# Making x with tokens on partitions and turning it by DMA transposes, in a fused linear-attention and bilinear feed-forward kernel

## The chip, the cores and the metric

One core of a Trainium2 chip runs the whole program. The metric is the device time of one execution in microseconds (us), by its median over several executions. All runs told here are of the fast state. Ratios are the mean time of one kernel's fast runs over that of the kernel before's fast runs of the same rounds, so they are not quite the ratio of the medians that I quote.

## The reference, cut to what matters

```python
def _attn_ref(q, k, v, g_norm):                      # 8 batches, 8 heads, 576 tokens, 64 dims
    kv = np.einsum('bhsd,bhse->bhde', k, v)
    out = np.einsum('bhsd,bhde->bhse', q, kv)
    rms = np.sqrt(np.mean(out * out, axis=-1, keepdims=True) + 1e-06)
    return out / rms * g_norm

def _moe_ref(x, w_a, w_b, w_out):                    # x: 4608 tokens x 512
    return ((x @ w_a) * (x @ w_b)) @ w_out           # 512 -> 1536 -> 512
```

x is the attention's output with the heads laid side by side. The feed-forward part contracts over x's 512 columns, so it wants x with columns on partitions and tokens along the free axis ("turned").

## The kernel before

Tokens go through the feed-forward part in nine strips of 512. While strip s (1 to 6) runs, the attention of batch s+1 is made between its matmuls, by `slot`. A step n below 12 of a strip is a unit: four matmuls for a, four for b, a ScalarE copy of a, a VectorE multiply of the two. Steps 12 to 15 are the output matmuls. x is made already turned, a pair of heads at a time, and so are its norms:

```python
        def x(self, p, i0):                      # x turned: columns on partitions
            for h in range(2):
                nc.tensor.matmul(P[:, i0 + h, 0:HF], lhsT=kvb[self.b % 2][:, p, :],
                                 rhs=self.qT[:, p, h * HF : (h + 1) * HF], start=True, stop=True)
        def psq(self, p, i0):                    # ScalarE: squares
            nc.scalar.activation(sq[p % 3], P[:, i0 : i0 + 2, 0:HF], AF.Square)
        def pss(self, p, i0, hs=(0, 1)):         # TensorE: sum over a head's 64 rows, on all rows
            for h in hs:
                nc.tensor.matmul(P[:, i0 + h, 0:HF], lhsT=ones, rhs=sq[p % 3][:, h, :], ...)
            ...                                  # ScalarE: 1/sqrt
        def pst(self, p, x0, hs=(0, 1)):         # VectorE: x * g * 1/rms
            ...
    def load_late(b):
        if b > EARLY:                            # GpSimd waits here for the q transpose of b-1
            nc.gpsimd.tensor_copy(gate, qT[(b - 1) % 2][0:1, 0, 0:1])
        ...                                      # six DMAs issued by GpSimd: q, k, v of batch b
    def transpose_q(b):
        nc.sync.dma_start_transpose(qT[b % 2], qs_d[b])
```

The sum over a head's rows runs across partitions, which is why it costs eight TensorE matmuls per batch.

Of the kernel before, what the change touches and what calls it, by code (L numbers as in the profile page):

```python
# [8 lines left out]
FP32 = mybir.dt.float32  # L9
BF16 = mybir.dt.bfloat16  # L10
AF = mybir.ActivationFunctionType
# [4 lines left out]
def kernel(  # L16
# [11 lines left out]
    nc = tc.nc  # L28

    B, H, S, D = q.shape  # L30
    d_model = H * D
    n_tok = B * S
    d_ff = moe_w_a.shape[1]
    KC = d_model // 128
    FC = d_ff // 128
    NP = H // 2
    HF = S // 2
    STRIP = 512
# [3 lines left out]
    EC, EP = 6, 96  # L42
# [6 lines left out]
    def sb(shape, dt, name):  # L49
        return pool.tile(shape, dt, name=name, tag=name)  # L50
# [11 lines left out]
    LC = S // 128  # L62
# [5 lines left out]
    kvs = [sb([128, NP, D], BF16, f"kvs{i}") for i in range(2)]  # L68

    kvb = [sb([128, NP, 128], BF16, f"kvb{i}") for i in range(2)]  # L70
    xt = [sb([128, n_tok], BF16, f"xt{i}") for i in range(KC)]
    abt = [[sb([128, STRIP], BF16, f"ab{i}_{f}") for f in range(FC)] for i in range(2)]
    a_sb = [sb([128, STRIP], BF16, f"asb{i}") for i in range(4)]
    sq = [sb([128, 2, HF], BF16, f"sq{i}") for i in range(3)]
    rs = [sb([128, 2, HF], FP32, f"rs{i}") for i in range(3)]
    o_sb = [sb([128, d_model], FP32, f"osb{i}") for i in range(4)]
    o_end = sb([128, d_model // 2], FP32, "o_end")
    ident = sb([128, 128], BF16, "ident")
# [3 lines left out]
    eps_t = sb([128, 1], FP32, "eps_t")  # L82
    warm = sb([128, 1], FP32, "warm")
    k32 = sb([EP, 2, EC, D], FP32, "k32")
    v32 = sb([EP, 2, EC, D], FP32, "v32")
    q32 = sb([EP, 2, EC, D], FP32, "q32")

    qc = sb([EP, EC, 2 * D], BF16, "qc")
    kc0 = sb([EP, EC, 2 * D], BF16, "kc0")
# [5 lines left out]
    P = psum.tile([128, 8, STRIP], FP32, name="P", tag="P")  # L95
# [27 lines left out]
    def load_late(b):  # L123
        if b > EARLY:

            nc.gpsimd.tensor_copy(gate, qT[(b - 1) % 2][0:1, 0, 0:1])  # L126
        d = qs_d[b].rearrange("t (h d) -> t h d", h=H)
        for hs in (slice(0, NP), slice(NP, H)):
            nc.gpsimd.dma_start(out=d[:, hs, :], in_=q[b, hs].rearrange("h t d -> t h d"))  # L129
        n = 128 * LC  # L130
        for t, src in ((ktl[b % 2], k), (vtl[b % 2], v)):
            nc.gpsimd.dma_start(
                out=t[:, :, 0:LC, :],
                in_=src[b, :, 0:n].rearrange("h (t c) d -> t h c d", c=LC),
            )
            nc.gpsimd.dma_start(
                out=t[0 : S - n, :, LC, :], in_=src[b, :, n:].rearrange("h t d -> t h d")
            )

    def transpose_q(b):  # L140
        nc.sync.dma_start_transpose(qT[b % 2], qs_d[b])


    class Attn:
# [75 lines left out]
        def pst(self, p, x0, hs=(0, 1)):  # L220
            for h in hs:
                t0 = self.b * S + h * HF
                nc.vector.scalar_tensor_tensor(  # L223
                    out=xt[p][:, t0 : t0 + HF],
                    in0=P[:, x0 + h, 0:HF],
                    scalar=g_col,
                    in1=rs[p % 3][:, h, :],
                    op0=ALU.mult,
                    op1=ALU.mult,
                )  # L230
# [10 lines left out]
                )  # L241


    class Unit:
        n = 0

# [5 lines left out]
        def mm(self, w, kcs):  # L252
            t0 = self.s * STRIP
            for kc in kcs:
                nc.tensor.matmul(  # L255
                    self.a if w is wa_t else self.b,
                    lhsT=w[:, kc, self.fc * 128 : (self.fc + 1) * 128],
                    rhs=xt[kc][:, t0 : t0 + STRIP],
                    start=(kc == KORD[0]),
                    stop=(kc == KORD[-1]),  # L260
                )
# [19 lines left out]
    def ffn_ab(s, fc, between=None):  # L281
        i = n_ab[0]
        n_ab[0] += 2
        u = Unit(s, fc, i % 3, (i + 1) % 3)
        u.part_a()
        if between:
            between()
        u.part_b()
# [38 lines left out]
    def ffn_o(s, g, i=O, between=None):  # L327
        o_mm(s, g, i, range(FC // 2))
        if between:
            between()  # L330
        o_mm(s, g, i, range(FC // 2, FC))
        o_out(s, g, i)
# [43 lines left out]
    X, SS = (4, 0), 6  # L376


    A = Attn(0)
# [9 lines left out]
    t = P[:, 2, :].bitcast(BF16)[:, 0:S].rearrange("q (c t) -> q c t", c=EC)  # L389
# [4 lines left out]
    for c in range(EC):  # L394
        nc.tensor.matmul(
            P[:, SS, 0 : 2 * D],
            lhsT=kc0[:, c, :],
            rhs=vc[:, c, :],
            start=(c == 0),
            stop=(c == EC - 1),  # L400
# [10 lines left out]
    for p in range(1, NP):  # L411
        i = X[p % 2]
# [38 lines left out]
    for fc in range(4, FC):  # L451
        ffn_ab(0, fc)


    A = Attn(1)
    h1, h2 = range(0, FC // 2), range(FC // 2, FC)
# [29 lines left out]
    def slot(A, s, n):  # L486

        kb = P[:, 7, 0 : NP * D].rearrange("q (p e) -> q p e", e=D)
        if s < 3:
            k0, xs, ss = 6, (7, 9.5, 12, 13.5), (8, 10.5, 12.5, 14)  # L490
        else:
            k0, xs, ss = 2, (4, 7, 10, 12), (5, 8, 11, 13)
        if n == k0:
            for p in range(NP):
                A.kv(p, kb[:, p, :])
            A.kv_out(slice(0, NP), kb)
        if n in xs:
            p = xs.index(n)
            A.x(p, X[0])
            A.psq(p, X[0])  # L500
        if n in ss:
            p = ss.index(n)
            A.pss(p, SS)
            A.pst(p, X[0])

    for s in range(1, N_STRIP - 1):
        b = s + 1
        A = Attn(b) if b < B else None
        for n in range(FC + 4):
            amid = (lambda n=n: slot(A, s, n - 0.5)) if A else None  # L510
            if n >= FC:
                i = O if n % 2 == 0 else n_ab[0] % 3
                n_ab[0] += n % 2
                ffn_o(s, n - FC, i, amid)
            elif s > 1 or n > 1:
                ffn_ab(s, n, amid)
            if A:
                slot(A, s, n)
            if n == 8 and b + 1 < B:
                if s > 1:  # L520
                    transpose_q(b + 1)
                    if b + 2 < B:
                        load_late(b + 2)
                else:
                    load_late(3)
        if s == 1:
            transpose_q(3)
            load_late(4)
# [43 lines left out]
```

## Time and profile before

| what | value | how to read it |
|---|---|---|
| median time | 322.1 us | 3 runs, 321.55 to 322.46, as known at the prediction; a fourth came with the result |
| span of the profiled run | 319.4 us | first to last instruction |
| TensorE busy | 98% | matmuls overlap, so take distances between starts |
| strip with attention | 33.90 us | strips 1 to 6, starts at 50.37, 84.27, 118.16 and so on |
| strip without | 31.08 us | strip 7 |
| GpSimd's issue of one batch's load | 7.2 us | nothing else runs on it meanwhile |

The lines themselves stand in the prediction below.

### The profile page before, as it was taken

What the parts mean: (1) busy time and instruction counts of PE and PEld (TensorE: products, weight loads), DVE (VectorE), ACT (ScalarE), POOL (GpSimd) and SP (SyncE); (2) the same over time, 40 slices, a digit from 0 to 9 for tenths busy, and PEclk for the clock granted to TensorE, in tenths of its full rate; (3) what the DMA queues carried; (4) which work ended last, traced back from release to release, by engine and by line L of the source; (5) the groups of instructions that cost most, each with busy time, mean ns of one, the idle gap of its engine ahead of it and who ended that gap; (6) DMA issues with size and microseconds to landing.
All of it is one profiled execution on the core that took longest, in us unless ns stands there. A gap on an engine that the chain in (4) does not pass through costs nothing.

```text
span 319.4 us, 4695 instructions
## 1 busy us (share of the span) xinstructions
PE 312.0 (98%) x1848; PEld 150.2 (47%) x1883; DVE 124.6 (39%) x218; ACT 125.3 (39%) x217; POOL 70.2 (22%) x94
## 2 busy tenths in 40 slices
PE   8899999999999999999999999999999999999995
PEld 3444454444445444444444444444544444444443
DVE  5543344444244333452245324532364243313421
ACT  3733165354335443542445225542454323123310
POOL 8944990070043080350070000000000000000000
PEclk9999999999999999999999999999999999999999
DMA  8999999999379999899499150003000200020002
GB/s 182 197 196 199 201 182 230 141 95 161 99 92 159 135 123 211 81 138 173 119 94 129 66 139 2 0 35 100 0 2 14 90 30 0 34 84 18 0 33 99
DMA packets 79308, 32.60 MB, mean 102 GB/s; under 512 B 49974, under 2 KB 74806, under 8 KB 79286
## 3 DMA queue, kind: packets, MB, share of 16 engines
q0 software_dynamic: 59120, 18.44, 53.0%
q1 hardware_dynamic: 19810, 13.44, 17.1%
q10 hardware_dynamic: 356, 0.43, 0.4%
q8 instruction: 14, 0.23, 0.3%
q14 instruction: 8, 0.07, 0.1%
HBM read 37.75 MB, written 12.98 MB: 159 GB/s over the span
## 4 chain that ended last, share of the span: by engine, by line
PE 93%; POOL 3%; DMA 2%; issue 1%; ACT 0%; POOLq 0%
PE P L255 58%; PE P L309 29%; PE P L209 2%; PE P L235 2%; DMA wb_t<-in_moe_w_b_dram 2%; PE P L158 2%; POOL vt L106 1%; POOL qt L106 1%; POOL kt L106 1%; PE P L182 0%; POOL wa_t L367 0%; POOL wb_t L367 0%; ACT o_end L540 0%; POOL ident masks.py:199 0%; POOL ident masks.py:197 0%
## 5 line engine op out<-in xcount | busy, mean ns | idle before, releaser
L273 DVE TENSOR_TENSOR ab<-P,asb 128x512 bf16<-128x512 f32 x108 | 74.5, 691 | 124.0 <-PE P L255 120.7
L255 PE MATMUL P<-xt,wa_t 128*128 128x512 bf16 x422 | 111.2, 379 | 0.9 <-issue 0.2
L255 PE MATMUL P<-xt,wb_t 128*128 128x512 bf16 x421 | 110.1, 379 | 0.3
L309 PE MATMUL P<-wo_t,ab 128*128 128x512 bf16 (+1 forms) x431 | 97.5, 373 | 0.7
L269 ACT CAST asb<-P 128x512 bf16<-128x512 f32 x108 | 63.0, 585 | 85.3 <-PE P L255 83.8
L255 PEld LDWEIGHTS <-wb_t 128*128 128x128 bf16 x432 | 42.3, 98 | 50.6 <-DMA wb_t<-in_moe_w_b_dram 0.5
L309 PEld LDWEIGHTS <-ab 128*128 128x128 bf16 x444 | 43.1, 98 | 45.4
L255 PEld LDWEIGHTS <-wa_t 128*128 128x128 bf16 x432 | 41.7, 98 | 45.1 <-issue 0.5
L223 DVE SCALAR_TENSOR_TENSOR xt<-P,g_col,rs 128x288 bf16<-128x288 f32 x64 | 30.1, 513 | 29.6 <-ACT rs L213 29.6
L205 ACT ACTIVATE sq<-P 128x576 bf16<-128x576 f32 x31 | 20.2, 650 | 25.1 <-PE P L235 23.2
L213 ACT ACTIVATE rs<-P,eps_t 128x576 f32<-128x576 f32 (+1 forms) x33 | 23.9, 727 | 14.9 <-PE P L209 14.6
L322 ACT COPY osb<-P 128x512 f32<-128x512 f32 x17 | 10.0, 586 | 46.0 <-PE P L309 43.6
L324 DVE COPY osb<-P 128x512 f32<-128x512 f32 x18 | 12.4, 691 | 26.9 <-PE P L309 26.8
L129 POOL DMA_DIRECT2D qs<-in_q_dram x12 | 19.6, 1636 | 2.2 <-issue 2.1
L126 POOL COPY gate<-qT 1x1 bf16<-1x1 bf16 x5 | 0.9, 176 | 83.2 <-DMA qT<-qs 83.2
L209 PE MATMUL P<-sq,ones 128*128 128x288 bf16 x64 | 13.2, 286 | 0.5 <-ACT sq L205 0.4
L235 PE MATMUL P<-qT,kvb 128*128 128x288 bf16 x56 | 11.4, 286 | 0.0
L169 ACT CAST kvb<-P 64x256 bf16<-64x256 f32 (+1 forms) x20 | 6.0, 301 | 11.1 <-PE P L158 11.0
L209 PEld LDWEIGHTS <-ones 128*128 128x128 bf16 x64 | 6.2, 98 | 7.5 <-issue 0.4
L235 PEld LDWEIGHTS <-kvb 128*128 128x128 bf16 x56 | 5.5, 98 | 6.0
L121 POOL DMA_DIRECT2D wo_t<-in_moe_w_out_dram x12 | 6.4, 530 | 6.7 <-DMA wb_t<-in_moe_w_b_dram 3.3
L337 PE MATMUL P<-zeros 128*128 128x512 bf16 x16 | 6.2, 532 | 1.2 <-DVE eps_t L352 1.2
(55 smaller groups left out, 82.6 us busy)
## 6 DMA issues: line engine op xcount, KB each, us to landing
out_dram<-osb SPq DMA_DIRECT2D x23, 256.0 KB, 2.0
qs<-in_q_dram POOLq DMA_DIRECT2D x12, 288.0 KB, 6.6
ktl<-in_k_dram POOLq DMA_DIRECT2D x6, 512.0 KB, 8.7
vtl<-in_v_dram POOLq DMA_DIRECT2D x6, 512.0 KB, 10.7
out_dram<-osb SPq DMA_DIRECT2D x13, 128.0 KB, 2.4
wo_t<-in_moe_w_out_dram POOLq DMA_DIRECT2D x12, 128.0 KB, 6.0
wa_t<-in_moe_w_a_dram POOLq DMA_DIRECT2D x5, 256.0 KB, 9.2
wb_t<-in_moe_w_b_dram POOLq DMA_DIRECT2D x5, 256.0 KB, 9.8
```

The lines of the kernel that those rows point to most:

```text
L129: nc.gpsimd.dma_start(out=d[:, hs, :], in_=q[b, hs].rearrange("h t d -> t h d"))
L205: nc.scalar.activation(sq[p % 3], P[:, i0 : i0 + 2, 0:HF], AF.Square)
L209: nc.tensor.matmul(P[:, i0 + h, 0:HF], lhsT=ones, rhs=sq[p % 3][:, h, :], start=True, stop=True)
L213: nc.scalar.activation(rs[p % 3][:, h0:h1, :], P[:, i0 + h0 : i0 + h1, 0:HF], AF.Abs_reciprocal_sqrt, bias=eps_t,)
L223: nc.vector.scalar_tensor_tensor(out=xt[p][:, t0 : t0 + HF], in0=P[:, x0 + h, 0:HF], scalar=g_col, in1=rs[p % 3][:, h, :], op0=ALU.mult, o ...
L235: nc.tensor.matmul(P[:, i0 + h, 0:HF], lhsT=kvb[self.b % 2][:, p, :], rhs=self.qT[:, p, h * HF : (h + 1) * HF], start=True, stop=True,)
L255: nc.tensor.matmul(self.a if w is wa_t else self.b, lhsT=w[:, kc, self.fc * 128 : (self.fc + 1) * 128], rhs=xt[kc][:, t0 : t0 + STRIP], st ...
L269: nc.scalar.copy(self.t, self.a)
L273: nc.vector.tensor_mul(abt[self.s % 2][self.fc], self.b, self.t)
L309: nc.tensor.matmul(P[:, i, e0:e1], lhsT=abt[s % 2][fc][:, g * 128 : (g + 1) * 128], rhs=wo_t[:, fc, e0:e1], start=(fc == 0), stop=(fc == F ...
L322: nc.scalar.copy(t, P[:, i, :])
L324: nc.vector.tensor_copy(t, P[:, i, :])
```

## The change

Its intent: with tokens on partitions, the sum over a head's 64 columns runs along the free axis. A VectorE reduce does it, and the eight sum matmuls go away; the x matmuls shrink to 128 columns. The price is that x comes out unturned, and a DMA transpose turns each chunk of 128 tokens. The core of the diff:

```diff
-    xt = [sb([128, n_tok], BF16, f"xt{i}") for i in range(KC)]
+    xt = sb([128, KC, n_tok], BF16, "xt")
...
+    q_x = sb([128, 2 * EC * D], FP32, "q_x")                  # q's first tile, used again
+    x_tok = q_x.bitcast(BF16).rearrange("p (c h d) -> p c h d", c=3, h=H)   # three buffers
...
+        def tx(self, c, i):
+            ...
+            for p in range(NP):
+                nc.tensor.matmul(P[0:n, i, p * 128 : (p + 1) * 128],
+                    lhsT=self.qT[:, p, t0 : t0 + n], rhs=kvb[self.b % 2][:, p, :], ...)
+            nc.scalar.activation(sqt[c % 2][0:n], P[0:n, i, :]..., AF.Square)
+        def tss(self, c):
+            nc.vector.reduce_sum(sst[c % 2][0:n], sqt[c % 2][0:n], axis=mybir.AxisListType.X)
+        def trs(self, c):
+            nc.scalar.activation(rst[c % 2][0:n], sst[c % 2][0:n], AF.Abs_reciprocal_sqrt, ...)
+            nc.gpsimd.tensor_mul(sqt[c % 2][0:n], <rst over columns>, <g_all over heads>)
+        def txt(self, c, i):
+            t = x_tok[:, c % 3]
+            nc.vector.tensor_mul(t[0:n], P[0:n, i, :]..., sqt[c % 2][0:n])
+            nc.sync.dma_start_transpose(xt[:, :, t0 : t0 + n], t[0:n]...)
...
+    nc.sync.dma_start(out=g_all, in_=g_norm.partition_broadcast(128))
...
-        if s < 3:
-            k0, xs, ss = 6, (7, 9.5, 12, 13.5), (8, 10.5, 12.5, 14)
-        else:
-            k0, xs, ss = 2, (4, 7, 10, 12), (5, 8, 11, 13)
+        k0 = {1: 5, 2: 3}.get(s, 2)
...
+        for c in range(LC + 1):                 # five chunks, one a unit
+            d = n - k0 - 1.5 - c
+            i = 4 + c % 3                       # three PSUM banks
+            # d == 0: tx, 0.5: tss, 1: trs, 2: txt
...
-            if n == 8 and b + 1 < B:            # (load_late(b + 2) at step 8; strip 1: load_late(3))
+            if s == 1 and n == 3:
+                load_late(3)
+            if s > 1 and b + 1 < B:
+                if n == 8:
+                    transpose_q(b + 1)
+                if n == 12 and b + 2 < B:
+                    load_late(b + 2)
```

`g_all` is the norm's weight on all partitions.

More of the change, by code (lines that the diff above doesn't have):

```diff
@@ L75 @@
     rs = [sb([128, 2, HF], FP32, f"rs{i}") for i in range(3)]
+    sqt = [sb([128, H, D], FP32, f"sqt{i}") for i in range(2)]
+    sst = [sb([128, H], FP32, f"sst{i}") for i in range(2)]
+    rst = [sb([128, H], FP32, f"rst{i}") for i in range(2)]
+    g_all = sb([128, D], FP32, "g_all")
     o_sb = [sb([128, d_model], FP32, f"osb{i}") for i in range(4)]
@@ L85 @@
     v32 = sb([EP, 2, EC, D], FP32, "v32")
-    q32 = sb([EP, 2, EC, D], FP32, "q32")
+    q_x = sb([128, 2 * EC * D], FP32, "q_x")
+    q32 = q_x[0:EP].rearrange("p (h c d) -> p h c d", h=2, c=EC)
+    x_tok = q_x.bitcast(BF16).rearrange("p (c h d) -> p c h d", c=3, h=H)
     qc = sb([EP, EC, 2 * D], BF16, "qc")
@@ L223, in pst @@
                 nc.vector.scalar_tensor_tensor(
-                    out=xt[p][:, t0 : t0 + HF],
+                    out=xt[:, p, t0 : t0 + HF],
                     in0=P[:, x0 + h, 0:HF],
@@ L241, in x @@
                 )
+        def tx(self, c, i):
+            t0 = c * 128
+            n = min(128, S - t0)
+            for p in range(NP):
+                nc.tensor.matmul(
+                    P[0:n, i, p * 128 : (p + 1) * 128],
+                    lhsT=self.qT[:, p, t0 : t0 + n],
+                    rhs=kvb[self.b % 2][:, p, :],
+                    start=True,
+                    stop=True,
+                )
+            nc.scalar.activation(
+                sqt[c % 2][0:n], P[0:n, i, :].rearrange("t (h d) -> t h d", h=H), AF.Square
+            )
+        def tss(self, c):
+            n = min(128, S - c * 128)
+            nc.vector.reduce_sum(sst[c % 2][0:n], sqt[c % 2][0:n], axis=mybir.AxisListType.X)
+        def trs(self, c):
+            n = min(128, S - c * 128)
+            nc.scalar.activation(
+                rst[c % 2][0:n],
+                sst[c % 2][0:n],
+                AF.Abs_reciprocal_sqrt,
+                bias=eps_t[0:n],
+                scale=1.0 / D,
+            )
+            nc.gpsimd.tensor_mul(
+                sqt[c % 2][0:n],
+                rst[c % 2][0:n].unsqueeze(2).to_broadcast([n, H, D]),
+                g_all[0:n].unsqueeze(1).to_broadcast([n, H, D]),
+            )
+        def txt(self, c, i):
+            t0 = c * 128
+            n = min(128, S - t0)
+            t = x_tok[:, c % 3]
+            nc.vector.tensor_mul(
+                t[0:n], P[0:n, i, :].rearrange("t (h d) -> t h d", h=H), sqt[c % 2][0:n]
+            )
+            t0 += self.b * S
+            nc.sync.dma_start_transpose(
+                xt[:, :, t0 : t0 + n], t[0:n].rearrange("t h d -> t (h d)")
+            )
     class Unit:
@@ L257, in mm @@
                     lhsT=w[:, kc, self.fc * 128 : (self.fc + 1) * 128],
-                    rhs=xt[kc][:, t0 : t0 + STRIP],
+                    rhs=xt[:, kc, t0 : t0 + STRIP],
                     start=(kc == KORD[0]),
@@ L496, in slot @@
             A.kv_out(slice(0, NP), kb)
-        if n in xs:
-            p = xs.index(n)
-            A.x(p, X[0])
-            A.psq(p, X[0])
-        if n in ss:
-            p = ss.index(n)
-            A.pss(p, SS)
-            A.pst(p, X[0])
+        for c in range(LC + 1):
+            d = n - k0 - 1.5 - c
+            i = 4 + c % 3
+            if d == 0:
+                A.tx(c, i)
+            elif d == 0.5:
+                A.tss(c)
+            elif d == 1:
+                A.trs(c)
+            elif d == 2:
+                A.txt(c, i)
     for s in range(1, N_STRIP - 1):
@@ L518 @@
                 slot(A, s, n)
-            if n == 8 and b + 1 < B:
-                if s > 1:
+            if s == 1 and n == 3:
+                load_late(3)
+            if s > 1 and b + 1 < B:
+                if n == 8:
                     transpose_q(b + 1)
-                    if b + 2 < B:
-                        load_late(b + 2)
-                else:
-                    load_late(3)
+                if n == 12 and b + 2 < B:
+                    load_late(b + 2)
         if s == 1:
```

## The prediction

> **What bounds the kernel now.** I read, in this order: the page's busy shares and its chain of work that ended last; the chain in order of time; the stretches table by strip (a strip is 512 tokens of the feed-forward part); the timelines of TensorE and of GpSimd.
>
> ```profile
> PE 312.0 (98%) x1848; PEld 150.2 (47%) x1883; DVE 124.6 (39%) x218; ACT 125.3 (39%) x217; POOL 70.2 (22%) x94
> ...
> PE 93%; POOL 3%; DMA 2%; issue 1%; ACT 0%; POOLq 0%
> ```
>
> TensorE is busy 98% and carries 93% of the chain; the rest is the start. So what counts is what TensorE issues, and whether it is made to wait. The stretches table has one row per strip; the first column is the strip's start and end, then its length:
>
> ```profile
> 118.33:152.22 33.89, 33.73 (x198) 16.28 (x200) 13.45 (x22) 14.39 (x24) 7.00 (x8) 1.00 1.26 151
> 152.22:186.12 33.90, 33.69 (x198) 16.29 (x200) 13.45 (x22) 14.39 (x24) 6.57 (x7) 1.00 0.73 102
> 253.92:285.00 31.08, 30.92 (x142) 14.10 (x144) 9.69 (x14) 8.19 (x14) 0.00 (x0) 1.00 0.09 35
> ```
>
> A strip that also carries the attention of the next batch takes 33.90 us, the strip without takes 31.08. Attention costs 2.82 us of a strip, and that is all that the change can touch. TensorE's timeline in such a strip (start, length, count) prices it:
>
> ```profile
> 123.44 0.82 PE L158 MATMUL P<-vtl,ktl 128*64 128x64 bf16 x40
> ...
> 125.93 1.03 PE L255 MATMUL P<-xt,wa_t 128*128 128x512 bf16 x4
> 126.79 1.03 PE L255 MATMUL P<-xt,wb_t 128*128 128x512 bf16 x4
> 127.66 0.41 PE L235 MATMUL P<-qT,kvb 128*128 128x288 bf16 x2
> 127.90 1.03 PE L255 MATMUL P<-xt,wa_t 128*128 128x512 bf16 x4
> ```
>
> Durations overlap, so I take starts. Eight 512-column matmuls start 1.73 us apart: 0.216 us each. Two 288-column ones take 127.90 - 127.66 = 0.24 us: 0.1225 each. The 40 of kv take 0.75 us to the next start (124.19). Check: 144 x 0.216 = 31.1; 16 x 0.1225 = 1.96 (8 for x, 8 for the sums of squares); 0.75; together 33.8 of 33.90. No gap is left, so TensorE waits for nobody in these strips.
>
> GpSimd's timeline at the load of batch 3, and 128-column matmuls that each have their own weights:
>
> ```profile
> 62.92 0.18 POOL L126 COPY gate<-qT 1x1 bf16<-1x1 bf16 x1 [15.02 <-DMA qT<-qs]
> 63.76 3.26 POOL L129 DMA_DIRECT2D qs<-in_q_dram  x2 [0.67 <-issue]
> 67.00 0.90 POOL L132 DMA_DIRECT2D ktl<-in_k_dram  x1
> 67.89 0.70 POOL L136 DMA_DIRECT2D ktl<-in_k_dram  x1
> 68.56 0.91 POOL L132 DMA_DIRECT2D vtl<-in_v_dram  x1
> 69.44 0.72 POOL L136 DMA_DIRECT2D vtl<-in_v_dram  x1
> ```
> ```profile
> 6.80 0.49 PE L395 MATMUL P<-vc,kc 96*128 96x128 bf16 x6 [0.18 <-ACT vc L387]
> ```
>
> GpSimd waits at its gate until the q transpose has landed, then spends 7.2 us issuing the load (62.92 to 70.16) and can do nothing else. The six 128-column matmuls last 0.49 us, of which the last lasts 0.218: (0.49 - 0.218) / 5 = 0.054 us from start to start, fresh weights included.
>
> **What the Trainium skill says.**
> 1. "TensorE: Matmul & The Clock Gate", section "Back-to-back issue gap": a lone matmul costs N/2.4 + 2.5 ns (56 ns for 128 columns), but about 81 ns for 128 and 131 ns for 512 in a stream of weight-load and matmul pairs. The trace has 216, 122.5 and 54 ns for 512, 288 and 128 columns, so it agrees with the formula and not with the stream figures. I take 0.056.
> 2. "GPSIMD Engine Reference", section 3.1: a two-input elementwise operation of 2048 fp32 takes 4497 ns. Scaled to 512 I estimate 1.2 us for the new multiply. No run here shows it yet. Section 4: two of GpSimd's cores make the descriptors of DMAs issued there, which agrees with the 7.2 us above.
> 3. "SBUF — State Buffer", section "Who interferes with whom": on trn2 a VectorE reduce never contends with GpSimd, nor does an instruction with at most one SBUF input. All new VectorE work is of those kinds. Nothing before shows it.
>
> **The change part by part.**
> Removed per batch from 2 to 7: 8 x-matmuls and 8 sum-matmuls, 16 x 0.1225 = 1.96 us of TensorE, all on the path; 4 squares of 650 ns and 4 roots of 741 ns on ScalarE (5.6 us); 8 VectorE multiplies of 513 ns (4.1 us).
>
> Added per batch: 5 chunks of tokens, each of 4 matmuls of 128 columns: 20 x 0.056 = 1.12 us of TensorE, on the path. The sums now go to a VectorE reduce, the norm to a small ScalarE root and a GpSimd multiply, x to a VectorE multiply out of PSUM, and the layout to a DMA transpose. Per chunk: VectorE 691 ns for the multiply (the row of the same shape, 128x512 out of PSUM) and an estimated 0.6 for the reduce (two copies of 512 and 256 columns take 691 and 426 ns, so 1.04 ns a column; 512 of them and some 60 ns); ScalarE an estimated 0.6 for the square (650 ns at 576 columns) and 0.2 for the root; GpSimd an estimated 1.2. All beside TensorE unless late.
>
> TensorE's ceiling on the gain: 6 x (1.96 - 1.12) = 5.0 us. I take off 0.5 for 30 new short groups between long matmuls (under 20 ns each, a choice): 4.5 us.
>
> Does the side work keep up? A unit (two groups of four matmuls) with a chunk lasts 1.73 + 0.22 = 1.95 us. In the three middle units VectorE has 0.69 + 0.69 + 0.6 = 1.98 us: just full. Following the first chunks by order: counting from the start of the unit with chunk 0, square done at 2.2, reduce at 3.4, root at 3.8, GpSimd at 5.1, x multiply about 5.4 to 6.1. Chunk 3 takes chunk 0's PSUM bank and wants it at 6.8. So 0.7 us of slack, and in the later strips no wait.
>
> In strip 1 GpSimd is not free. load_late(3) is now placed at step 3, ahead of the multiplies, but its gate still waits for q of batch 2, 62.92 us, so GpSimd issues until 70.16 and then multiplies until 71.4. In the old trace kv starts at 62.62; it is a unit earlier now, so chunk 0 runs at about 64.3, its root is there at 67, and chunk 3 wants the bank at about 70.2. The x multiply ends 71.4 + 0.1 + 0.7 = 72.2. TensorE waits about 2.1 us. In strip 2 the same load of batch 4 ends (98.7 in the old trace, shifted 1.4 by the above) at about 100.1; multiply and x end 102.1, bank wanted 101.9: 0.3 us. From strip 3 on the load is issued at step 12, past the multiplies: nothing.
>
> DMA transposes: q's 576x512 takes 4.8 to 11.2 us to land and 2.2 to 6.2 us of the queue's issue, so 128x512 should take an estimated 2 to 4 us. Strip s+1 wants its first chunks 7 units (13 us) after their issue or more. In strip 2 the q transpose of batch 4 stands ahead of chunk 2 on the same queue and waits for its load until about 104, so chunk 2 lands near 114, wanted at 119. Hidden.
>
> Sum: -4.5 + 2.1 + 0.3 = -2.1 us: 322.1 becomes 320.0 us.
>
> **The rivals.**
> A. Short matmuls are dearer than the formula. At 81 ns, 20 of them cost 1.62 us: the gain is 6 x 0.34 = 2.0, and with the 2.4 us of waits the result is 322.5. For: the skill's stream figure. Against: 54 ns in this trace, but only in one group of six.
> B. VectorE becomes the bound in the middle units. It is full by my sum, with 0.7 us of slack; a multiply of GpSimd above 2.2 us, or each of about eight hand-overs costing 0.1 us more than I counted, turns into a wait of 0.3 to 1 us in each of six strips: 322 to 326.
> C. Transposes come late: x at the start of strip 3, or a chunk's buffer held so long that VectorE stops. For: shares of 1.08 and 1.26 of DMA in strips 2 and 3, and a queue in order. Against: margins of 5 us and more. A wait of 3 us twice would give 326.
> D. No wait in strip 1, because the q transpose lands earlier or the multiply is not held: 317.5.
>
> **Range and chances.** A, B and C only add, D subtracts 2.4. I predict 320.0 us, 317.3 to 323.0 eight times in ten. 2% is 6.4 us. Faster than 315.7 is beyond TensorE's 5.0 us, so 2%. Slower than 328.5 needs over 8 us of waits beyond mine: C badly wrong, or B in all strips at over 1.4 us; 5%. Within 2%: 93%.
>
> **What would show it.** Right: strips 3 to 6 last 33.0 to 33.2 us, chunk groups take 0.22 to 0.25 us; strip 1 has one wait of about 2 us, on VectorE's x multiply of chunk 0, which itself waits for GpSimd behind the load; no wait of TensorE for a DMA past the start. Wrong: strips of 33.5 or more with waits for VectorE (B) or without (A), a strip start that waits for a transpose (C), or GpSimd free at 67 us (D).

## The result

The changed kernel takes 323.88 us (323.3 to 324.25, 4 runs) against 321.83 (321.3 to 322.46, 4 runs); the ratio is 1.0061, 95% interval 1.0036 to 1.0087. So it is 0.6% slower, and 0.9 us above the top of my range.

From the changed kernel's page, the busy shares and the chain that ended last:

```profile
PE 311.9 (97%) x1907; PEld 147.4 (46%) x1907; DVE 138.3 (43%) x230; ACT 116.5 (36%) x229; POOL 101.5 (32%) x124
...
PE 70%; DMA 19%; POOL 7%; issue 3%; DVE 1%; ACT 0%; POOLq 0%; DVEq 0%; ACTq 0%
```

In the lines of the changed kernel, L310 is a matmul of a or b, L256 of x, L364 of the output, L328 VectorE's multiply of a and b, L290 its x multiply, L379 its copy of an output.

TensorE had 93% of the chain before and has 70% now: 19% has gone to DMA. Busy TensorE time has not fallen (312.0 to 311.9), but that sum counts overlapping durations: a matmul of x lasts 0.22 us though the next starts 0.056 us after it. So it hides the gain. The strips show it; the stretches of strips 1, 2, 3 and 7 (behind the length stand the busy times of TensorE, its weight loads, VectorE, ScalarE and GpSimd; at the end the granted clock, the DMA share and GB/s):

```profile
52.22:87.79 35.57, 33.79 (x206) 15.88 (x204) 16.69 (x27) 13.33 (x27) 11.75 (x12) 1.00 1.17 152
87.79:123.45 35.66, 33.78 (x205) 15.71 (x204) 15.62 (x24) 12.71 (x26) 18.47 (x19) 1.00 1.19 146
123.45:156.73 33.28, 33.28 (x205) 15.79 (x204) 15.72 (x24) 12.93 (x26) 11.85 (x12) 1.00 0.92 121
...
256.57:287.65 31.08, 31.08 (x146) 14.07 (x145) 9.68 (x14) 8.21 (x14) 0.00 (x0) 1.00 0.10 35
```

The first column holds each strip's start, and that gives the account of the two profiled spans (319.4 and 322.3 us):

| stretch | before | after | difference | I had predicted |
|---|---|---|---|---|
| to the start of strip 1 | 50.37 | 52.22 | +1.85 | 0 |
| strip 1 | 33.90 | 35.57 | +1.67 | -0.75 + 2.1 = +1.35 |
| strip 2 | 33.89 | 35.66 | +1.77 | -0.75 + 0.3 = -0.45 |
| strips 3 to 6 | 4 x 33.90 | 4 x 33.28 | -2.48 | -3.0 |
| rest | 65.6 | 65.7 | +0.1 | 0 |
| sum | | | +2.9 | -2.1 |

(My 4.5 us of gain over six strips is 0.75 each.) The mechanism works where nothing disturbs it: 0.62 us a strip. Three things take it back. First, TensorE's timeline around the first chunk of strip 3, which is the undisturbed case:

```profile
131.22 1.03 PE L310 MATMUL P<-xt,wa_t 128*128 128x512 bf16 x4
132.08 0.39 PE L256 MATMUL P<-kvb,qT 128*128 128x128 bf16 x4
132.30 1.03 PE L310 MATMUL P<-xt,wb_t 128*128 128x512 bf16 x4
```

From start to start the four short matmuls take 132.30 - 132.08 = 0.22 us, so 0.056 each, with fresh weights each time. That holds for the four chunks of 128 tokens. The fifth chunk has 64 tokens, so its weights have 64 columns:

```profile
139.02 1.03 PE L310 MATMUL P<-xt,wa_t 128*128 128x512 bf16 x4
139.97 0.41 PE L256 MATMUL P<-kvb,qT 128*64 128x128 bf16 x4
140.32 1.04 PE L310 MATMUL P<-xt,wb_t 128*128 128x512 bf16 x4
```

From 139.02 to 140.32 are 1.30 us, of which the four long matmuls take 0.86. So this group costs 0.44 us, twice as much as each of the others. And here are TensorE's waits in strips 1 and 2; the bracket at the end of a line is the idle time before it and what ended it:

```profile
73.63 0.38 PE L256 MATMUL P<-kvb,qT 128*128 128x128 bf16 x4 [1.29 <-DVE q_x L290]
...
82.61 5.34 PE L364 MATMUL P<-wo_t,ab 128*128 128x512 bf16 x24 [0.38 <-DVE osb L379]
...
104.61 0.38 PE L256 MATMUL P<-kvb,qT 128*128 128x128 bf16 x4 [0.46 <-DVE q_x L290]
...
114.27 0.39 PE L364 MATMUL P<-wo_t,ab 128*128 128x512 bf16 x1 [0.63 <-DVE ab L328]
115.46 8.16 PE L364 MATMUL P<-wo_t,ab 128*128 128x512 bf16 x37 [0.80 <-DVE ab L328]
```

All five name VectorE, but VectorE is only the messenger. Its own waits tell two kinds apart. The waits at 73.63 and 104.61 are for the fourth chunk's PSUM bank, and VectorE's multiply of the first chunk, which frees that bank, waits for GpSimd. In strip 1:

```profile
72.89 0.69 DVE L290 TENSOR_TENSOR q_x<-P,sqt 128x512 bf16<-128x512 f32 x1 [1.97 <-POOL sqt L280]
```

GpSimd's timeline there is:

```profile
64.55 0.18 POOL L134 COPY gate<-qT 1x1 bf16<-1x1 bf16 x1 [14.80 <-DMA qT<-qs]
65.39 3.26 POOL L137 DMA_DIRECT2D qs<-in_q_dram  x2 [0.67 <-issue]
...
71.06 0.72 POOL L144 DMA_DIRECT2D vtl<-in_v_dram  x1
71.76 2.08 POOL L280 TENSOR_TENSOR sqt<-rst,g_all 128x512 f32<-128x512 f32 x2
```

GpSimd goes from the load straight into two multiplies, back to back: they were due and stood in line. This is the predicted wait. The other three follow on a wait of VectorE that I had not in my sum. VectorE, for the fourth chunk's x in strip 1 and in strip 2:

```profile
81.27 0.69 DVE L290 TENSOR_TENSOR q_x<-P,sqt 128x512 bf16<-128x512 f32 x1 [2.28 <-DMA xt<-q_x]
...
112.92 0.69 DVE L290 TENSOR_TENSOR q_x<-P,sqt 128x512 bf16<-128x512 f32 x1 [2.95 <-DMA xt<-q_x]
```

The multiply writes a token buffer (q_x), and that buffer's last transpose (xt<-q_x) has not landed. The trace's row on the tokens' transposes (from issue to landing: least, median, most), in strip 1 of the changed kernel:

```profile
DMA to landing us min/median/max: 2.5/6.3/7.6
```

The same row from strip 3 on, where a batch's load is issued only behind all five transposes of the strip, or not at all:

```profile
DMA to landing us min/median/max: 2.3/2.4/4.0
```

The third thing is the start. In the timeline of SyncE's queue of the changed kernel the load of g_all is third:

```profile
1.68 0.45 SPq L509 DMA_DIRECT2D g_all<-in_g_norm_dram  x1
```

GpSimd's ninth DMA, in its timeline of the changed kernel:

```profile
8.59 0.63 POOL L114 DMA_DIRECT2D vt<-in_v_dram  x1 [1.88 <-DMA qt<-in_q_dram]
```

and in that of the kernel before:

```profile
6.90 0.63 POOL L106 DMA_DIRECT2D vt<-in_v_dram  x1
```

By the trace the ninth DMA waits for the first of eight to land, and all weights come behind it: GpSimd is 1.7 us late from there on.

### The profile page after: what moved, and what is told of

It is laid out like the page before. It is cut to its first block, busy times and chain, and to the rows that moved or that the text cites. A ratio compares the mean times of both kernels' runs of the same rounds, so it can differ in the third digit from the quotient of the medians.

```text
span 322.3 us, 4938 instructions
## 1 busy us (share of the span) xinstructions
PE 311.9 (97%) x1907; PEld 147.4 (46%) x1907; DVE 138.3 (43%) x230; ACT 116.5 (36%) x229; POOL 101.5 (32%) x124
## 4 chain that ended last, share of the span: by engine, by line
PE 70%; DMA 19%; POOL 7%; issue 3%; DVE 1%; ACT 0%; POOLq 0%; DVEq 0%; ACTq 0%
PE P L310 40%; PE P L364 26%; DMA wb_t<-in_moe_w_b_dram 5%; DMA qT<-qs 5%; DMA xt<-q_x 4%; DMA qt<-in_q_dram 2%; DMA vt<-in_v_dram 2%; PE P L256 2%; POOL qs L137 1%; PE P L166 1%; POOL wo_t L129 1%; POOL sqt L280 1%; POOL ktl L140 1%; POOL vtl L140 1%; DVE q_x L290 0%
## 5 line engine op out<-in xcount | busy, mean ns | idle before, releaser
L328 DVE TENSOR_TENSOR ab<-P,asb 128x512 bf16<-128x512 f32 x108 | 74.4, 690 | 105.2 <-PE P L310 97.3
L310 PE MATMUL P<-xt,wb_t 128*128 128x512 bf16 x432 | 111.8, 379 | 0.3 <-DMA wb_t<-in_moe_w_b_dram 0.3
L310 PE MATMUL P<-xt,wa_t 128*128 128x512 bf16 x432 | 111.9, 379 | 0.0
L364 PE MATMUL P<-wo_t,ab 128*128 128x512 bf16 (+1 forms) x444 | 96.1, 373 | 1.8 <-DVE ab L328 1.4
L364 PEld LDWEIGHTS <-ab 128*128 128x128 bf16 x444 | 43.0, 98 | 51.5 <-DVE ab L328 2.2
L310 PEld LDWEIGHTS <-wa_t 128*128 128x128 bf16 x432 | 41.7, 98 | 49.6 <-issue 0.5
L310 PEld LDWEIGHTS <-wb_t 128*128 128x128 bf16 x432 | 40.8, 98 | 45.0 <-DMA wb_t<-in_moe_w_b_dram 0.9
L280 POOL TENSOR_TENSOR sqt<-rst,g_all 128x512 f32<-128x512 f32 (+1 forms) x30 | 31.2, 1047 | 88.6 <-ACT rst L273 88.6
L379 DVE COPY osb<-P 128x512 f32<-128x512 f32 x18 | 12.4, 691 | 47.1 <-PE P L364 40.6
L290 DVE TENSOR_TENSOR q_x<-P,sqt 128x512 bf16<-128x512 f32 (+1 forms) x30 | 20.4, 681 | 9.7 <-DMA xt<-q_x 5.2
L263 ACT ACTIVATE sqt<-P 128x512 f32<-128x512 f32 (+1 forms) x30 | 17.8, 593 | 9.6 <-DVE q_x L290 8.2
L269 DVE TENSOR_REDUCE sst<-sqt 128x8 f32<-128x512 f32 (+1 forms) x30 | 20.4, 679 | 0.8
L256 PEld LDWEIGHTS <-qT 128*128 128x128 bf16 (+1 forms) x120 | 8.9, 100 | 10.3 <-issue 4.9
L256 PE MATMUL P<-kvb,qT 128*128 128x128 bf16 (+1 forms) x120 | 11.7, 220 | 1.7 <-DVE q_x L290 1.7
L273 ACT ACTIVATE rst<-sst,eps_t 128x8 f32<-128x8 f32 (+1 forms) x30 | 9.0, 301 | 2.4 <-DVE sst L269 2.1
L231 DVE SCALAR_TENSOR_TENSOR xt<-P,g_col,rs 128x288 bf16<-128x288 f32 x16 | 7.5, 512 | 5.4 <-ACT rs L221 5.4
```

What stands on the lines that cost most here:

```text
L256: nc.tensor.matmul(P[0:n, i, p * 128 : (p + 1) * 128], lhsT=self.qT[:, p, t0 : t0 + n], rhs=kvb[self.b % 2][:, p, :], start=True, stop=True,)
L263: nc.scalar.activation(sqt[c % 2][0:n], P[0:n, i, :].rearrange("t (h d) -> t h d", h=H), AF.Square)
L269: nc.vector.reduce_sum(sst[c % 2][0:n], sqt[c % 2][0:n], axis=mybir.AxisListType.X)
L280: nc.gpsimd.tensor_mul(sqt[c % 2][0:n], rst[c % 2][0:n].unsqueeze(2).to_broadcast([n, H, D]), g_all[0:n].unsqueeze(1).to_broadcast([n, H, D]),
L290: nc.vector.tensor_mul(t[0:n], P[0:n, i, :].rearrange("t (h d) -> t h d", h=H), sqt[c % 2][0:n])
L310: nc.tensor.matmul(self.a if w is wa_t else self.b, lhsT=w[:, kc, self.fc * 128 : (self.fc + 1) * 128], rhs=xt[:, kc, t0 : t0 + STRIP], st ...
```

## The experiments

Theory after the result: three costs, each apart from TensorE's gain. (1) The load of g_all delays the first loads. (2) Three token buffers are too few while a batch's load slows the transposes. (3) GpSimd's load issue holds its multiplies. Rivals are told with each run. Since the kernel before measured 321.4 to 321.5 us in these rounds and 321.8 in those of the changed kernel, I compare ratios to it; the changed kernel's 1.0061 is 323.4 us in these terms. Its interval, 1.0036 to 1.0087, is 0.8 us either way, so a difference of some 1 us to it is not clear of noise; for such I go by the waits and strips in the profiles. The runs k0_seven, tx_twice and g_front_warm were made on chip 12, the other eight on chip 9; for the two kernels compared above the record names no chip.

| run | median us (lowest to highest) | ratio to before | strip 1 starts | strip 1 | strip 2 |
|---|---|---|---|---|---|
| changed kernel | 323.88 (323.3 to 324.25) | 1.0061 | 52.22 | 35.57 | 35.66 |
| g_late | 322.52 (322.0 to 322.91) | 1.0030 | 50.66 | 35.99 | 34.82 |
| five_bufs | 321.58 (321.33 to 322.58) | 1.0011 | 55.34 | 33.28 | 33.27 |
| before_g_front | 324.52 (322.55 to 326.14) | 1.0103 | 52.49 | 33.90 | 33.89 |
| k0_later | 323.15 (320.11 to 324.28) | 1.0042 | 51.52 | 33.74 | 38.43 |
| g_bufs | 320.65 (319.5 to 320.79) | 0.9964 | 50.70 | 35.80 | 33.59 |
| all_three | 318.56 (317.51 to 318.97) | 0.9899 | 50.76 | 34.33 | 33.28 |
| no_gate3 | 322.66 (321.92 to 323.46) | 1.0038 | 52.02 | 35.00 | 34.91 |
| q_behind | 324.96 (323.98 to 325.44) | 1.0105 | 54.94 | 33.28 | 35.14 |
| k0_seven | 317.90 (317.58 to 318.09) | 0.9889 | 50.60 | 33.28 | 33.28 |
| tx_twice | 324.61 (324.3 to 324.81) | 1.0098 | 50.95 | 34.39 | 34.40 |
| g_front_warm | 322.91 (322.35 to 323.05) | 1.0042 | 52.33 | 33.90 | 33.90 |

The last three columns are of each run's one profiled execution; strips 3 to 6 last 33.28 in all forms of the changed kernel but tx_twice. All results were correct.

### The load of g_all moved (g_late), and put into the kernel before (before_g_front)

```diff
 # g_late: in the changed kernel
-    nc.sync.dma_start(out=g_all, in_=g_norm.partition_broadcast(128))       # third on SyncE
     nc.sync.dma_start(out=gate_d, in_=vt[1][0:1, H - 1, EC - 1, D - 1 : D]) # waits for batch 1
+    nc.sync.dma_start(out=g_all, in_=g_norm.partition_broadcast(128))
 # before_g_front: in the kernel before, used by nobody
+    g_all = sb([128, D], FP32, "g_all")
+    nc.sync.dma_start(out=g_all, in_=g_norm.partition_broadcast(128))
```

> The changed kernel, with the load of g_all (128 rows of 256 bytes) issued behind the gate of batch 1 instead of third on SyncE's queue at the start. Theory: that load delays the first loads of q, k and v, GpSimd's ninth DMA then waits for the first one to land, and everything after is 1.7 to 1.9 us late. Expected: strip 1 starts at 50.4 us as in the kernel before (52.2 in the changed kernel), the time falls by 1.6 to 1.9 us against the changed kernel, to about 322.1 us. Rival (the late start comes from the shared tile of q and the tokens, or is chance): no change, 323.9 us.

> The kernel before, with the load of g_all added third on SyncE's queue and used by nobody. Theory: it costs what the changed kernel loses at the start, 1.6 to 1.9 us: about 323.6 us, with GpSimd's ninth DMA waiting near 2 us for the first one. Rival: a 32 KB load is hidden, 321.8 us.

The start of strip 1 moved as expected both ways: 52.22 to 50.66 without the load, 50.37 to 52.49 with it, and GpSimd's ninth DMA waited 2.17 us in the latter. So the load of 32 KB is shown to cost about 1.6 to 2.1 us of the start. Two things missed. g_late gave only 0.3% (1.0 us) of time by the ratios. That is not clear of noise (1.0018 to 1.0042 against 1.0036 to 1.0087), and the profiled spans fell by 2.0 us, from 322.3 to 320.3. Strip 1 did grow, from 35.57 to 35.99: TensorE waits 0.69 us for v of batch 2 there, which it now reaches 1.6 us earlier. Strip 2 fell, from 35.66 to 34.82. And before_g_front took 324.5 us with a spread of 3.6 us, where the kernel before spreads 0.5. That spread is taken up further down.

### Five token buffers (five_bufs)

```diff
+    v_x = sb([128, 2 * EC * D], FP32, "v_x")           # v's first tile, used again like q's
-    x_tok = q_x.bitcast(BF16).rearrange(..., c=3, h=H)
+    x_tok = [t.bitcast(BF16).rearrange(..., c=3, h=H) for t in (q_x, v_x)]
-            t = x_tok[:, c % 3]
+            t = x_tok[c // 3][:, c % 3]
```

> The changed kernel, with five token buffers for x (three in q's old tile, two in v's) instead of three. Theory: VectorE is held in strips 1 and 2 because the fourth and fifth chunk wait for a buffer whose DMA transpose has not landed (5.2 us of waits), and TensorE then waits 0.5 us for VectorE in strip 1 and 0.6 + 0.8 us in strip 2. Expected: no wait of VectorE for a transpose, those three waits of TensorE gone, 1.5 to 2.0 us less, about 322.0 us. Rival (the buffers are not what holds, the wait only moves to GpSimd or to the next reader): under 0.5 us less.

The ratio fell from 1.0061 to 1.0011, 1.6 us, as the theory said, and no x multiply waits for a transpose. The profile can't be used for more: its start was 3.1 us later than the changed kernel's (the clock fell, see g_front_warm below), and with loads that far ahead even the waits for GpSimd are gone. g_bufs below is the clean form.

### x of strips 1 and 2 one unit later (k0_later)

```diff
-        k0 = {1: 5, 2: 3}.get(s, 2)
+        k0 = {1: 6, 2: 4}.get(s, 2)
```

> The changed kernel, with kv and x of strips 1 and 2 begun one unit later, so that GpSimd has issued its load when the first chunk needs its multiply. Theory (GpSimd is the cause of the waits of 1.3 us in strip 1 and 0.5 us in strip 2 at the fourth chunk): these two go; the waits for transposes further on stay or grow by up to 0.5 us each since the chunks stand later: 0.8 to 1.7 us less, about 322.6 us. Rival (waits only move, since VectorE is full): within 0.4 us of the changed kernel.

The fourth chunk's wait in strip 1 fell from 1.29 to 0.30 us and that of strip 2 went, so GpSimd's load issue is their cause. But TensorE now waits 3.13 us in one piece in strip 2, behind a VectorE that waits 3.95 and 1.51 us for transposes: the chunks moved into the thick of the load. In time nothing is shown: the ratio is 1.0042 (1.0011 to 1.0073), not clear of the changed kernel's, and the granted clock was below full in all six runs (0.984 to 0.995). Taking away one cost alone feeds another.

### Both the late g_all and five buffers (g_bufs), and all three edits (all_three)

> The changed kernel with both edits: the load of g_all behind the gate, and five token buffers. Theory (three separate costs: the front load, the buffers, GpSimd's load issue): the start and the waits for transposes go, the wait for GpSimd at the fourth chunk of strip 1 (1.25 us) and of strip 2 (up to 0.5) stays. Expected: the kernel before less 6 x 0.62 plus 1.3 to 2.2, so 319.1 to 320.0 us, and no wait of VectorE for a transpose. Rival (an early start only meets the loads earlier and gives its gain back, as strip 1 with the late g_all hints, 35.99 us against 35.57): 321 us or more.

> As the kernel with both edits, and kv and x of strips 1 and 2 one unit later. Theory: the wait for GpSimd's load issue goes too; strips 1 and 2 last 33.3 to 33.6 us; the whole 318.0 to 318.8 us. Rival (the wait moves to the end of the strips, as when x was moved alone, 3.1 us there): no better than with both edits alone.

g_bufs is 0.6 us slower than the top of its range: the x multiplies' waits for transposes are gone and strip 2 lasts 33.59, but strip 1 has a wait of 0.91 us for v of batch 2 beside the 1.18 us for GpSimd. So the rival holds in part: an earlier start meets the loads earlier. all_three came out within its range in time, but strip 1 with 34.33 did not come down to 33.6: a wait of 0.89 us for GpSimd is left. Its stretches of strips 1 and 2:

```profile
50.76:85.09 34.33, 33.44 (x206) 15.80 (x204) 16.79 (x27) 13.44 (x27) 11.76 (x12) 1.00 1.23 164
85.09:118.37 33.28, 33.28 (x205) 15.80 (x204) 15.77 (x24) 12.93 (x26) 18.50 (x19) 1.00 1.19 133
```

Strip 2 is at 33.28 with the same share of DMA (1.19) as in the changed kernel: the traffic is still there, and no longer matters once no buffer waits for it.

### No gate ahead of batch 3's load (no_gate3)

```diff
-        if b > EARLY:
+        if b > EARLY + 1:
```

> The changed kernel without GpSimd's wait for the q transpose of batch 2 ahead of the load of batch 3 (it writes other buffers, so nothing is at stake but time). GpSimd then issues that load from about 50 us on and is free when the first chunk wants its multiply. Theory (it is the issuing that holds TensorE 1.3 us in strip 1): that wait goes, if q of batch 2 does not land more than 1.5 us later; strip 1 falls from 35.6 to 33.5 to 34.3 us. Rival (the load's traffic is what counts): q of batch 2, or the tokens' transposes, land later and strip 1 stays at 35 us or more.

GpSimd had issued the load by 60.3 us and TensorE's 1.29 us wait for the fourth chunk went, which is the second independent sign that the issuing was its cause. In its place TensorE waited 0.91 us for v and 0.46 us for q of batch 2, which the early load had slowed. Strip 1 lasted 35.00: both sides were right, the theory on the wait and the rival on the time.

The run shows one thing more, on the transposes. With the load out of their way, those of strip 1 landed after

```profile
DMA to landing us min/median/max: 2.4/2.5/3.7
```

instead of 2.5/6.3/7.6, and VectorE's wait of 2.28 us for them went. In strip 2, where a load still runs beside them, they took up to 7.0 us and VectorE waited 3.20.

### The q transpose of batch 4 behind the tokens' (q_behind)

```diff
-                if n == 8:
+                if n == (11 if s == 2 else 8):
                     transpose_q(b + 1)
```

> The changed kernel with the q transpose of batch 4 put behind the five token transposes of strip 2 on SyncE's queue. Theory (in strip 2 that transpose, 5 us of issue and on the same queue, holds the tokens' transposes back, and so the buffers): VectorE's wait of 3 us for a transpose in strip 2 and TensorE's 0.6 + 0.8 us after it go; 1.0 to 1.5 us less, about 322.6 us. Rival (the load's traffic alone makes the transposes slow, 6.8 us against 2.4): the waits stay within 0.5 us of what they were.

The rival was right. VectorE in strip 2 of this run, at the fourth chunk:

```profile
112.83 0.69 DVE L290 TENSOR_TENSOR q_x<-P,sqt 128x512 bf16<-128x512 f32 x1 [2.88 <-DMA xt<-q_x]
```

It waited 2.88 us, against 2.95 with the q transpose ahead, and TensorE's waits after it were 0.56 and 0.80. So the queue's order is not the cause. The slow transposes are those that run beside a batch's load. That the load is their cause is shown for strip 1 by no_gate3, which moved the load away from them. For strip 2 I take it from this run and the rows of landings; no run moved the load there. This run's time is not comparable, since its start was slow (strip 1 at 54.94), which leads to the next point.

### The spread of the front load (g_front_warm)

The page of q_behind has in its row of granted clock, in 40 slices of 8 us:

```profile
PEclk9589999999999999999999999999999999999999
```

The clock was at half in the second slice and a part of the third (0.50 in each microsecond from 9 to 18). five_bufs' trace shows the same from 10 to 19. In both, TensorE had waited 1.3 to 1.4 us for q at 7 to 9 us. The wait alone doesn't decide: the profiled run of before_g_front has one of 1.32 us at the same place, and its clock stayed at 1.00. The test is to fill that wait in before_g_front:

```diff
+    dummy(6, 7)          # six matmuls of zeros into an idle PSUM bank
     A.qtr(1, 3)
```

> The kernel before with the unused load of g_all at the front, and six dummy matmuls more where TensorE waits for q of pair 1 (1.3 us). Theory: the load's large spread (322.6 to 326.1 us) comes from the granted clock, which fell to 0.5 for 8 us in two profiles with that load after TensorE had idled at the start; with TensorE kept busy there no run is above 324, and the median is near 323.0 us. Rival (the spread comes from the loads themselves): runs above 324.5 us are as frequent as before, 2 of 3.

Five runs lie between 322.35 and 323.05, where without the six matmuls four of six were above 324. So the front load costs twice: 1.5 us each time by the median of g_front_warm (2.0 at the start of strip 1), and in some runs up to some 3 us more when the clock drops. The first is shown. For the second, the record lists each run's mean granted clock: the four runs of before_g_front above 324 us had 0.984 to 0.989, its two below had 1.0, and the five of g_front_warm had 0.998 to 1.0. So the longer runs are those with a lowered clock. That the idle time lowers it, and the six matmuls prevent it, is likely but not shown: g_front_warm ran on another chip (12, not 9), and before_g_front was not run there.

### One unit later still (k0_seven), and the short matmuls doubled (tx_twice)

```diff
 # k0_seven, on all_three
-        k0 = {1: 6, 2: 4}.get(s, 2)
+        k0 = {1: 7, 2: 4}.get(s, 2)
 # tx_twice, on all_three
-            for p in range(NP):
+            for p in [p for p in range(NP) for _ in range(2)]:
```

> As the kernel with all three edits, with kv and x of strip 1 yet one unit later. Theory: the last wait for GpSimd (0.89 us in strip 1) goes, strip 1 falls from 34.3 to 33.3 us, the whole from 318.6 to about 317.6 us, and the kernel before less 6 x 0.62 = 317.8 is reached. Rival (chunks so late in strip 1 meet the output part and the next strip's start): a new wait there, 318.5 us or more.

> As the kernel with all three edits, each 128-column matmul of x issued twice. Theory (TensorE alone sets the later strips, and such a matmul costs 0.056 us): strips 3 to 6 grow by 20 x 0.056 = 1.12 us, from 33.28 to 34.40, and the whole by about 6.5 us to 325. Rival (VectorE sets the units with chunks, as it is full by my sum): under 0.6 us a strip.

k0_seven has all six strips at 33.28, no wait left in them, and 317.90 us: 1.1% below the kernel before (interval 0.9876 to 0.9903), and 1.7% below the changed kernel by the ratios. 6 x 0.62 = 3.7 us is what TensorE's own work offers, and 3.5 of it arrived. In tx_twice strips 2 to 6 grew from 33.28 to 34.40, 1.12 us for 20 more matmuls: 0.056 each. The fifth chunk's group, now of eight, takes 0.66 us (136.20 to 137.72, less 0.86 for four long ones), so the 0.21 us that it costs beyond 0.056 for each matmul come once a group; why, no run shows. So TensorE alone sets the strips, and VectorE, full as it is in three units, doesn't.

## Why the prediction was wrong, point by point

- **TensorE's part** was right in mechanism and nearly in size. In the chunks of 128 tokens short matmuls cost 0.056 us (predicted 0.056), and nothing more for standing between long ones, for which I had taken off 0.5 us. The gain per strip was 0.62 us where I had 0.75, because I priced the fifth chunk, of 64 tokens, like the others: its group took 0.44 us and not 0.22. That is the whole of 0.84 - 0.62 = 0.22 us a strip, 1.3 us in all.
- **"Does the side work keep up?"** was right: GpSimd's multiply took 1.04 us (estimate 1.2), the reduce 0.68 (0.6; the two copies that I named, of 691 and 426 ns, leave 161 ns beside the columns and so give 0.69), the root 0.30 (0.2), and no wait came in strips 3 to 6. Rival B did not happen.
- **"In strip 1 GpSimd is not free"** was right: 1.29 us of idle time before the fourth chunk's matmuls (1.46 counted from start to start) against 2.1 predicted, and 0.46 (0.6) in strip 2 against 0.3. The chain was the predicted one, the gate, the issue, the multiply, the x multiply, the PSUM bank. k0_later and no_gate3 confirm it. That strip 1 still came within 0.3 us of the forecast is luck: the wait was 0.6 us shorter than predicted, and 0.54 us behind the transposes (82.61, from start to start) and 0.3 us in kv, which took 1.05 us for 0.75, filled the place.
- **"DMA transposes: ... 2 to 4 us ... Hidden"** failed, on two counts. The size held only away from the loads: 2.3 to 4.0 us there, up to 7.6 beside them. And I checked the wrong deadline. I asked when the next strip reads x (7 units later) and not when the buffer is written again (three chunks later, about 6 us). Rival C named "a chunk's buffer held so long that VectorE stops" and dismissed it with a margin that belonged to the other deadline. In strip 2 this is most of the miss of 2.2 us.
- **The load of g_all** was in no step. I worked through what the change adds inside the strips and took the start as unchanged: +1.85 us, almost as much as the whole forecast gain. The order of SyncE's instructions, which I had, shows it third in the queue without a wait.
- **Rival D** (no wait in strip 1) did not happen; neither did A.

In sum, 322.1 - 2.1 missed a start of 1.85 us, 2.2 in strip 2, 0.3 in strip 1, and 0.5 of gain in strips 3 to 6: 4.9 of the 5.0 us between the predicted -2.1 and the profiled +2.9.

## What to carry to other kernels

For each buffer that an added transfer reads, ask when it is written next, and take the transfer's time from a stretch with the same traffic, not from an idle one. Look where an added load really stands in its queue: a small one without a wait can run, as here, beside the first loads at the program's start. Where several waits lean on one another, remove them together before judging the idea: the three edits gave -1.0, -1.6 and -0.6 us alone, of which only the second is clear of noise, and about -5.2 us as a set, by the ratios.

## What the Trainium skill lacked or had wrong

- "TensorE: Matmul & The Clock Gate", section "Back-to-back issue gap": the stream figures of 81 ns for 128 columns and 131 ns for 512 do not hold here. tx_twice shows 1.12 us for 20 matmuls of 128 columns with fresh weights (56 ns), and 512 columns take 216 ns; the page's formula for a lone matmul fits both.
- The same page, section "What's actually happening", gives at least one idle window, about 3.4 us, before the clock falls to half. In q_behind and five_bufs the granted clock was 0.50 from 10 to 15 us though the longest wait of TensorE just before was 1.31 and 1.38 us. A wait of 1.32 us in before_g_front's profile left it at 1.00.
- "DMA: Bandwidth & Descriptors", section "DMA Transpose (X-bar)", has no time for a small transpose from SBUF to SBUF. Here 128x512 bf16 took 1.2 us of the queue's issue, and landed after 2.3 to 2.5 us alone and up to 7.6 us beside a load of GpSimd (8.5 in g_bufs).
- No page that I read prices a load that broadcasts one row to 128 partitions: 32 KB took 5.8 us to land at the start, and cost strip 1's start 1.6 to 2.1 us.
- "GPSIMD Engine Reference", section 4, says who makes the descriptors but not what it holds up: the six DMAs of one batch held GpSimd for 7.2 us, and a multiply whose input was ready at 69.3 us began at 71.76. The figure of its section 3.1 for elementwise work, scaled to 1.2 us (an estimate; 1.12 in straight proportion), stands against 1.04 us measured.
- The claim of "SBUF — State Buffer", section "Who interferes with whom", that a VectorE reduce doesn't contend with GpSimd is neither shown nor refuted here: in the changed kernel's trace a reduce and a multiply of GpSimd overlap by 0.25 us at most (136.00 to 136.25). Its other claim that I used, on instructions with at most one SBUF input, the page makes only outside VectorE's 2-port performance modes, a condition that I left out.
